# Attention followed by two feed-forward blocks: another order of TensorE's work within a pair of heads, and the low part of x on another engine

## The chip, the cores and the metric

The kernel runs on one core of a Trainium2 chip. The metric is the device time of one execution in microseconds (us), the median of several runs. A profiled execution has its own time and, a little shorter, its span, from the first to the last instruction in the trace.

## The reference

The inputs are q, k and v of shape (2, 12, 448, 64) in float32, a number cap, and four weight matrices in float64. Cut to what matters:

```
scores = cap * tanh(q @ k.T / sqrt(64) / cap)        # each batch and head
attn   = softmax(scores)                              # exp, divided by the row's sum
x      = (attn @ v), heads side by side               # 896 x 768
x      = elu(x @ w_in1) @ w_out1                      # 768 -> 2048 -> 768
out    = relu(x @ w_in2) ** 2 @ w_out2                # 768 -> 2048 -> 768
```

## The kernel before, in words

Every float32 operand of a matrix product is split into a high and a low part (tiles whose names end in h and l), and a product is the sum of three matmuls: high by high, high by low, low by high.

The attention takes the 24 heads as 12 pairs, one iteration of the loop at L505 for each pair n. The 448 keys make three full blocks of 128 per head and a last block that both heads share: seven slots, which `PARTS` (L214) divides into a first part (slots 0 to 3) and a second part (slots 4 to 6). The steps of a pair:

- `turn(n)`, TensorE: eight transposes of k and q into the PSUM tile `pt` (one buffer). `high(n)`, ScalarE: its high part `kqh`. `low(n)`, VectorE: its low part `kql`; for odd n, it also issues the loads of a later group's k and q.
- `scores(n, c)`, TensorE: for c = 0 to 2 six matmuls of 64 rows each, for c = 3 three of 128, into the PSUM tile `sc` (two buffers). `tanh(n, c)`, ScalarE, frees that buffer.
- `exp(n, i)`, ScalarE, in place on part i of the tile `e`.
- `split_p(n, i)`, VectorE: a cast to `ph` (L228) and a subtraction to `pl` (L229). Tile p has one buffer: the first part of a pair waits until all value products of the pair before have read it.
- `prep_v(n)`, GpSimd: for each head a cast (L149) and a subtraction (L150), then a cast (L153) and a subtraction (L154) for the shared block.
- `pv(n, i)`, TensorE: the value products of part i, twelve matmuls each, into the PSUM tile `po` (one buffer). The order of terms is `ph` with `vh`, `ph` with `vl`, `pl` with `vh`. A column of ones in v makes the row sums too.
- `pv_out(n)`, ScalarE copies `po` out, and a DMA fetches the row of sums (`den`). `norm(n)`: VectorE takes the reciprocal (L271), and DMAs write it to DRAM (`far`) and read it back into 64 partitions (`bc`).
- `norm_x(n)`: VectorE multiplies (L291, two instructions of 64 partitions), casts to `xh` (L297), and GpSimd subtracts to `xl` (L298).

All instructions are issued in the order written by hand (`manual_schedule`); each engine, and the DMA queue of SyncE (SP), takes its own in that order. Semaphores order them between engines. In iteration n the engines' orders before are:

- TensorE: `pv(n-1, 1)`, `scores(n, 2)`, `scores(n, 3)`, `pv(n, 0)`, `scores(n+1, 0)`, `scores(n+1, 1)`, `turn(n+2)`
- ScalarE: `tanh(n, 0)`, `high(n+1)`, `tanh(n, 1)`, `exp(n, 0)`, `pv_out(n-1)`, `tanh(n, 2)`, `tanh(n, 3)`, `exp(n, 1)`
- VectorE: `split_p(n-1, 1)`, `low(n+1)`, `norm(n-2)`, `split_p(n, 0)`, `norm_x(n-3)`
- GpSimd: `prep_v(n+1)`, the low part of `norm_x(n-3)`

In iterations 0 and 1 VectorE also prepares the first pieces of w_in1. After the loop come the last value products, mixed with the first products of the feed-forward part, which is TensorE's work for the rest of the time.

Of the kernel before, what the change touches and what calls it, by code (L numbers as in the profile page):

```python
# [26 lines left out]
def attention_moe_kernel(  # L27
# [12 lines left out]
    nc = tc.nc  # L40
# [100 lines left out]
    def prep_v(n):  # L141
        if n >= len(pairs):
            return
        g, pp = divmod(n, 2)
        vh, vl = vhs[n % 2], vls[n % 2]
        for hh in range(2):
            vn = nat[g]["v"][:, 2 * pp + hh]
            h, l = (t[:, hh:NB - 1:2, :D] for t in (vh, vl))
            nc.gpsimd.tensor_copy(h, vn)  # L149
            nc.gpsimd.tensor_tensor(l, vn, h.bitcast(F32), op=ALU.subtract)  # L150
        vn = nat[g]["w"][:, pp]
        h, l = (t[:, NB - 1, :D] for t in (vh, vl))
        nc.gpsimd.tensor_copy(h, vn)  # L153
        nc.gpsimd.tensor_tensor(l, vn, h.bitcast(F32), op=ALU.subtract)  # L154
# [4 lines left out]
    def turn(n):  # L159
        if n >= len(pairs):  # L160
            return
        g, pp = divmod(n, 2)
        hs = slice(2 * pp, 2 * pp + 2)
        pt = ps1.tile([P, 2, W], F32, name="pt", tag="pt")
        for u, src in enumerate("kq"):
            for c in range(NFULL):
                nc.tensor.transpose(  # L167
                    pt[:, u, c * P:(c + 1) * P],
                    nat[g][src][:, c, hs].rearrange("p h d -> p (h d)"),
                    ident,  # L170
                )
            z = kzs[g % 2][:, pp] if u == 0 else qzs[g % 2][:, hs].rearrange("p h d -> p (h d)")
            nc.tensor.transpose(pt[:, u, NFULL * P:], z, ident)
        st["pt", n] = pt

    def high(n, copy=nc.scalar.copy):
        if n >= len(pairs):
            return
        st["qk", n] = [ap_.tile([P, 2, W], F32R, name=x, tag=x) for x in ("kqh", "kql")]
        copy(st["qk", n][0], st["pt", n])  # L180

    def low(n):
        if n >= len(pairs):
            return
        h, l = st["qk", n]
        nc.vector.tensor_tensor(l, st["pt", n], h.bitcast(F32), op=ALU.subtract)
        if n % 2:
            load_group(n // 2 + 2, "kq")

    def scores(n, c):  # L190

        if n >= len(pairs):
            return
        h, l = st["qk", n]
        sc = psc.tile([P, 2, W], F32, name="sc", tag="sc")
        terms = ((h, h), (h, l), (l, h))
        last = len(terms) - 1
        ks = slice(c * P, (c + 1) * P)
        for i, (kt, qt) in enumerate(terms):
            for u, r in enumerate(ROWS if c < NFULL else (slice(0, P),)):  # L200
                nc.tensor.matmul(  # L201
                    sc[:, u, :S], kt[r, 0, ks], qt[r, 1, :S], start=i == 0, stop=i == last
                )
        st["sc", n, c] = sc

    def tanh(n, c):
        if c == 0:
            st["e", n] = ap_.tile([P, NB, S], F32, name="e", tag="e")
        w = 2 if c < NFULL else 1
        nc.scalar.activation(  # L210
            st["e", n][:, 2 * c:2 * c + w], st["sc", n, c][:, :w, :S], AF.Tanh, scale=tsc
        )
# [3 lines left out]
    def exp(n, i):  # L216
        e = st["e", n][:, PARTS[i]]
        nc.scalar.activation(e, e, AF.Exp, scale=capt)  # L218

    def split_p(n, i, copy=nc.vector.tensor_copy):  # L220
        if n < 0:
            return
        if i == 0:
            st["p", n] = [
                ap_.tile([P, NB, S], F32R, name=x, tag=x, bufs=1) for x in ("ph", "pl")
            ]
        e, h, l = (t[:, PARTS[i]] for t in [st["e", n]] + st["p", n])
        copy(h, e)  # L228
        nc.vector.tensor_tensor(l, e, h.bitcast(F32), op=ALU.subtract)  # L229

    def pv(n, i):


        if n < 0:
            return
        if i == 0:
            st["po", n] = ps1.tile([P, 2, W], F32, name="po", tag="po")
        po = st["po", n]
        ph, pl = st["p", n]
        vh, vl = vhs[n % 2], vls[n % 2]  # L240
        terms = ((vh, ph), (vl, ph), (vh, pl))
        mms = [
            (s % 2, slice(0, P), s, x)
            for x in terms for s in range(NB - 1)[PARTS[i]]
        ]
        if i == 1:
            mms += [(u, r, NB - 1, x) for x in terms for u, r in enumerate(ROWS)]
        for j, (u, r, s, (vt, pt)) in enumerate(mms):
            nc.tensor.matmul(  # L249
                po[:, u, :S], vt[r, s], pt[r, s],  # L250
                start=i == 0 and j < 2, stop=i == 1 and j >= len(mms) - 2,
            )

    def pv_out(n, copy=nc.scalar.copy):
        if n < 0:
            return
        pvs = ap_.tile([P, 2, S], F32, name="pvs", tag="pvs", bufs=3)
        copy(pvs, st["po", n][:, :, :S])
        st["pvs", n] = pvs
        den = ap_.tile([D, 2 * S // D], F32, name="den", tag="den")  # L260
        nc.sync.dma_start(den, pvs[D:D + 1].rearrange("p h s -> p (h s)"))
        st["den", n] = den

    def norm(n):


        if n < 0:
            return
        den = st["den", n]
        rd = ap_.tile([D, 2 * S // D], F32, name="rd", tag="rd")  # L270
        nc.vector.reciprocal(rd, den)  # L271
        far = dp.tile([D, 2 * S // D], F32, name="far", tag="far")
        nc.sync.dma_start(far, rd)
        bc = ap_.tile([D, 2, S], F32, name="bc", tag="bc")
        flat = far.rearrange("p s -> (p s)")
        for u in range(2):
            src = flat[u * S:(u + 1) * S].unsqueeze(0).to_broadcast([D, S])
            nc.sync.dma_start(bc[:, u], src)
        st["bc", n] = bc

    def norm_x(n, copy=nc.vector.tensor_copy, low=nc.gpsimd):

        if n < 0:
            return []
        b, hp = pairs[n]
        xn = ap_.tile([P, S], F32, name="xn", tag="xn")
        hi, lo = xh[:, hp, b * S:(b + 1) * S], xl[:, hp, b * S:(b + 1) * S]

        def x():
            for u, r in enumerate(ROWS):  # L290
                nc.vector.tensor_tensor(  # L291
                    xn[r], st["pvs", n][:D, u], st["bc", n][:, u], op=ALU.mult
                )

        return [
            x,
            lambda: copy(hi, xn),  # L297
            lambda: low.tensor_tensor(lo, xn, hi.bitcast(F32), op=ALU.subtract),  # L298
        ]
# [133 lines left out]
    def emit(steps):  # L433
        for step in steps:
            step()
# [42 lines left out]
    with tc.manual_schedule():  # L478
# [26 lines left out]
        for n in range(np_):  # L505
            last = n == np_ - 1
            tanh(n, 0)
            high(n + 1)
            tanh(n, 1)
            split_p(n - 1, 1)  # L510
            exp(n, 0)
            low(n + 1)
            pv(n - 1, 1)
            scores(n, 2)
            scores(n, 3)
            pv_out(n - 1)
            norm(n - 2)
            tanh(n, 2)
            tanh(n, 3)
            exp(n, 1)  # L520
            prep_v(n + 1)
            split_p(n, 0)
            pv(n, 0)
            scores(n + 1, 0)
            scores(n + 1, 1)
            turn(n + 2)
            emit(norm_x(n - 3))
            if n % 2 == 0:
                load_group(n // 2 + 2, "v")

            if n == 0:
                emit(ws.start())
            if n < 2:
                emit(ws.advance())
            if n == 1:
                ws.settle()
# [192 lines left out]
```

## Time and profile before

| what | value |
|---|---|
| median of 3 runs | 622.38 us (621.15 to 623.63) |
| the profiled execution: its time, its span | 621.61 us, 619.8 us |
| busy share of the span: TensorE, VectorE, ScalarE, GpSimd | 94%, 70%, 54%, 13% |
| the same, TensorE, over 95.2 to 105.8 us | 9.04 us of 10.6 |
| mean granted TensorE clock, share of full speed | 0.992 |

The shares are means over the whole span. The attention lies in about the first 146 us of it, the feed-forward blocks in the rest; for one pair of heads, a stretch such as that of the fourth row is to be read. Matmuls are pipelined and their ends are modelled, so TensorE's busy time is not time at its peak rate. A row's duration is an instruction's own, and two neighbours on an engine may overlap by a little, so for sums on one engine the distance between starts is used.

### The profile page before, as it was taken

Reading aid. Unit: us, or ns where it says so; the run is one execution under the profiler, and the core shown is the slowest. Engines: PE = TensorE matmul, PEld = TensorE weight load, DVE = VectorE, ACT = ScalarE, POOL = GpSimd, SP = SyncE. Lnnn points to the kernel's source line nnn. Section 1 sums busy time; section 2 is a strip of 40 time slices with the busy share of each in tenths; the row PEclk is TensorE's granted clock in tenths of the full one; section 3 lists DMA queues with packets and bytes.
Section 4 is the critical chain, followed back from the end, with each engine's and each line's share of the span. In section 5 each row is a group of like instructions: output and inputs, shape, how many; then the busy total and the mean of one; then the engine's idle time right before and its main releaser. Section 6 shows DMA issues by size and latency. Waiting matters only on the chain.

```text
span 619.8 us, 8625 instructions
## 1 busy us (share of the span) xinstructions
PE 585.3 (94%) x3036; PEld 522.5 (84%) x3036; DVE 433.9 (70%) x822; ACT 335.9 (54%) x482; POOL 79.2 (13%) x111
## 2 busy tenths in 40 slices
PE   5788888888899999999999999999999999999997
PEld 3556566656799999999999999999999999999997
DVE  1797888889799888866656666776776779992000
ACT  2777878783498777753332333656666655441000
POOL 1753444432000000000000000000000011231000
PEclk9799999999899999999999999999999999999999
DMA  4853340103444433324333343433334436632000
GB/s 113 215 127 88 79 116 21 30 17 107 144 127 129 128 102 117 96 65 133 104 124 96 112 128 102 128 104 120 108 102 124 119 94 187 186 108 102 22 23 34
DMA packets 82988, 64.76 MB, mean 104 GB/s; under 512 B 38656, under 2 KB 78848, under 8 KB 82944
## 3 DMA queue, kind: packets, MB, share of 16 engines
q1 hardware_dynamic: 82944, 64.20, 35.6%
q8 instruction: 24, 0.39, 0.3%
q14 instruction: 20, 0.16, 0.1%
HBM read 61.34 MB, written 2.80 MB: 103 GB/s over the span
## 4 chain that ended last, share of the span: by engine, by line
PE 81%; DVE 7%; ACT 6%; DMA 2%; SPq 2%; issue 1%; POOL 0%; DVEq 0%; ACTq 0%; POOLq 0%
PE acc L465 18%; PE acc L466 18%; PE acc L464 18%; PE acc L660 6%; PE acc L661 6%; PE acc L659 6%; DVE pl L229 4%; PE po L249 3%; ACT e L218 3%; PE sc L201 2%; DVE ph L228 2%; ACT kqh L180 1%; ACT e L210 1%; PE pt L167 1%; SPq L116 1%
## 5 line engine op out<-in xcount | busy, mean ns | idle before, releaser
L464 PE MATMUL acc<-xh,wh 128*128 128x448 f32 x384 | 140.5, 366 | 3.9 <-ACT wh L407 2.0
L465 PE MATMUL acc<-xl,wh 128*128 128x448 f32 x384 | 140.6, 366 | 0.2 <-DVE xl L298 0.2
L466 PE MATMUL acc<-xh,wl 128*128 128x448 f32 x384 | 140.3, 365 | 0.0
L407 ACT CAST wh<-wf 128x384 fp32r<-128x384 f32 (+2 forms) x114 | 57.8, 507 | 103.4 <-PE acc L465 87.5
L353 ACT ACTIVATE wf<-wst 128x384 f32<-128x384 f32 (+2 forms) x130 | 70.5, 543 | 63.8 <-DVE wl L402 34.4
L402 DVE TENSOR_TENSOR wl<-wf,wh 128x384 fp32r<-128x384 f32 (+2 forms) x116 | 63.6, 548 | 56.1 <-ACT wh L407 56.0
L464 PEld LDWEIGHTS acc<-xh,wh 128*128 128x128 f32 x384 | 72.6, 189 | 10.9 <-ACT wh L407 2.7
L466 PEld LDWEIGHTS acc<-xh,wl 128*128 128x128 f32 x384 | 72.5, 189 | 6.0 <-DVE wl L402 0.7
L465 PEld LDWEIGHTS acc<-xl,wh 128*128 128x128 f32 x384 | 72.5, 189 | 5.5 <-DVE xl L298 0.5
L394 DVE SCALAR_TENSOR_TENSOR wf<-wst,wf 128x384 uint32<-128x384 uint32 (+3 forms) x132 | 71.2, 539 | 0.0
L387 DVE SCALAR_TENSOR_TENSOR wf<-wst,wf 128x384 uint32<-128x384 uint32 (+3 forms) x132 | 71.0, 538 | 0.0
L465 PE MATMUL acc<-gl,wh 128*128 128x448 f32 x192 | 70.0, 365 | 0.0
L466 PE MATMUL acc<-gh,wl 128*128 128x448 f32 x192 | 70.0, 364 | 0.0
L464 PE MATMUL acc<-gh,wh 128*128 128x448 f32 x192 | 69.8, 364 | 0.0
L402 POOL TENSOR_TENSOR late<-wf,late 128x336 fp32r<-128x336 f32 x16 | 15.2, 951 | 388.3 <-ACT late L407 388.3
L366 DVE TENSOR_SCALAR wf<-wf 128x384 uint32<-128x384 uint32 (+3 forms) x132 | 54.4, 412 | 0.6
L210 ACT ACTIVATE e<-sc,tsc 128x896 f32<-128x896 f32 (+1 forms) x48 | 42.6, 917 | 21.8 <-PE sc L201 21.8
L362 DVE TENSOR_SCALAR wf<-wf 128x384 f32<-128x384 f32 (+3 forms) x132 | 46.7, 353 | 8.0 <-ACT wf L353 7.9
L229 DVE TENSOR_TENSOR pl<-e,ph 128x1792 fp32r<-128x1792 f32 (+1 forms) x24 | 51.0, 2125 | 1.6
L646 DVE COPY o<-acc 128x432 f32<-128x432 f32 (+1 forms) x8 | 4.5, 557 | 53.9 <-PE acc L661 47.7
L660 PE MATMUL acc<-wl,gh 128*128 128x432 f32 x112 | 40.3, 359 | 0.0
L661 PE MATMUL acc<-wh,gl 128*128 128x432 f32 x112 | 40.1, 358 | 0.0
(77 smaller groups left out, 993.8 us busy)
## 6 DMA issues: line engine op xcount, KB each, us to landing
wst<-in_moe_w_in_dram SPq DMA_DIRECT2D x64, 384.0 KB, 3.2
wst<-in_moe_w_out_dram SPq DMA_DIRECT2D x24, 384.0 KB, 3.2
wst<-in_moe_w_out_dram SPq DMA_DIRECT2D x16, 432.0 KB, 3.3
wst<-in_moe_w_out_dram SPq DMA_DIRECT2D x16, 336.0 KB, 2.9
wst<-in_moe_w_out_dram SPq DMA_DIRECT2D x12, 256.0 KB, 2.7
bc<-far SPq DMA_DIRECT2D x24, 112.0 KB, 2.9
v<-in_v_dram SPq DMA_DIRECT2D x24, 96.0 KB, 2.6
k<-in_k_dram SPq DMA_DIRECT2D x15, 128.0 KB, 2.7
```

The source lines that it names most:

```text
L229: nc.vector.tensor_tensor(l, e, h.bitcast(F32), op=ALU.subtract)
L353: nc.scalar.activation(self.f[i], hi.bitcast(F32), AF.Abs)
L366: v.tensor_scalar(fb, fb, 3, 0x3FFFFFFF, op0=ALU.logical_shift_left, op1=ALU.bitwise_and)
L387: v.scalar_tensor_tensor(out=fb, in0=hi, scalar=0xC0000000, in1=fb, op0=ALU.bitwise_and, op1=ALU.bitwise_or,)
L394: v.scalar_tensor_tensor(out=fb, in0=lo, scalar=29, in1=fb, op0=ALU.logical_shift_right, op1=ALU.bitwise_or,)
L402: (v if dst is None else nc.gpsimd).tensor_tensor(wl, self.f[i], wh.bitcast(F32), op=ALU.subtract)
L407: (v.tensor_copy if self.alone else nc.scalar.copy)(wh, self.f[i])
L464: nc.tensor.matmul(acc, w[0], x[0], start=first, stop=False)
L465: nc.tensor.matmul(acc, w[0], x[1], start=False, stop=False)
L466: nc.tensor.matmul(acc, w[1], x[0], start=False, stop=last)
L660: nc.tensor.matmul(acc, gh[:, f, gs], w[1], start=False, stop=False)
L661: nc.tensor.matmul(acc, gl[:, f, gs], w[0], start=False, stop=z)
```

## The change

In iteration n, `scores(n, 2)` goes ahead of `pv(n-1, 1)`, and `turn(n+2)` from the end of the iteration to behind `scores(n, 3)`. `scores(n+1, 0)` and `scores(n+1, 1)` go ahead of `pv(n, 0)`. `norm_x(n-3)` goes from behind to ahead of `split_p(n, 0)`, and its subtraction to `xl` from GpSimd to VectorE. ScalarE's order is as it was.

```
             low(n + 1)
+            scores(n, 2)
             pv(n - 1, 1)
-            scores(n, 2)
             scores(n, 3)
+            turn(n + 2)
             pv_out(n - 1)
             norm(n - 2)
             tanh(n, 2)
             tanh(n, 3)
             exp(n, 1)
             prep_v(n + 1)
+            emit(norm_x(n - 3, low=nc.vector))
             split_p(n, 0)
-            pv(n, 0)
             scores(n + 1, 0)
             scores(n + 1, 1)
-            turn(n + 2)
-            emit(norm_x(n - 3))
+            pv(n, 0)
             if n % 2 == 0:
                 load_group(n // 2 + 2, "v")
```

## Rows read from the trace of the kernel before

**Rows 1.** Windows: engines' busy us, TensorE clock (PEclk), DMA share; three stretches.
```profile
19.00:24.00 5.00, 4.45 (x12) 3.81 (x12) 4.79 (x9) 2.96 (x5) 3.06 (x3) 0.50 0.74 167
...
95.20:105.80 10.60, 9.04 (x54) 6.49 (x53) 9.08 (x10) 8.34 (x9) 4.72 (x8) 1.00 0.07 22
...
200.00:600.00 400.00, 400.00 (x2046) 376.40 (x2046) 272.15 (x598) 196.07 (x325) 15.19 (x16) 1.00 0.36 110
```

**Rows 2.** Chain that ended last, one pair: start us, us, what.
```profile
87.54 1.08 PE po L249 x4
88.62 1.42 PE sc L201 x10
...
91.11 1.02 ACT kqh L180
92.12 0.91 ACT e L210
93.06 1.80 ACT e L218
```

**Rows 3.** Timeline of VectorE, one period: start, us, operation, [idle before it].
```profile
94.89 1.12 DVE L228 CAST ph<-e 128x1792 fp32r<-128x1792 f32 x1 [1.33 <-ACT e L218]
96.11 2.02 DVE L229 TENSOR_TENSOR pl<-e,ph 128x1792 fp32r<-128x1792 f32 x1
98.05 1.26 DVE L291 TENSOR_TENSOR xn<-pvs,bc 64x448 f32<-64x448 f32 x2
99.34 0.39 DVE L297 CAST xh<-xn 128x448 fp32r<-128x448 f32 x1
99.65 0.85 DVE L228 CAST ph<-e 128x1344 fp32r<-128x1344 f32 x1
100.54 2.40 DVE L229 TENSOR_TENSOR pl<-e,ph 128x1344 fp32r<-128x1344 f32 x1
102.86 1.21 DVE L186 TENSOR_TENSOR kql<-pt,kqh 128x1024 fp32r<-128x1024 f32 x1
103.99 0.22 DVE L271 RECIPROCAL rd<-den 64x14 f32<-64x14 f32 x1
105.53 1.12 DVE L228 CAST ph<-e 128x1792 fp32r<-128x1792 f32 x1 [1.32 <-ACT e L218]
```

**Rows 4.** Timeline of VectorE, four instructions elsewhere.
```profile
38.19 1.56 DVE L229 TENSOR_TENSOR pl<-e,ph 128x1344 fp32r<-128x1344 f32 x1
...
42.70 2.23 DVE L229 TENSOR_TENSOR pl<-e,ph 128x1792 fp32r<-128x1792 f32 x1
...
52.33 1.09 DVE L228 CAST ph<-e 128x1792 fp32r<-128x1792 f32 x1 [1.37 <-ACT e L218]
...
136.32 1.09 DVE L228 CAST ph<-e 128x1792 fp32r<-128x1792 f32 x1 [1.30 <-PE po L249]
```

**Rows 5.** Timeline of GpSimd, four instructions.
```profile
41.73 1.32 POOL L150 TENSOR_TENSOR vl<-v,vh 128x192 fp32r<-128x192 f32 x1
...
99.82 1.71 POOL L298 TENSOR_TENSOR xl<-xn,xh 128x448 fp32r<-128x448 f32 x1 [3.63 <-DVE xh L297]
103.53 0.34 POOL L149 CAST vh<-v 128x192 fp32r<-128x192 f32 x1 [2.01 <-PE po L249]
103.95 0.60 POOL L150 TENSOR_TENSOR vl<-v,vh 128x192 fp32r<-128x192 f32 x1
```

**Rows 6.** Line L298 on VectorE: ns min/median/max, start, form.
```profile
L298 DVE TENSOR_TENSOR xl<-xn,xh x1: 626/626/626, 160.5 to 160.5; 128x448 fp32r<-128x448 f32 x1
```

**Rows 7.** Timeline of the DMA queue of SP, two issues.
```profile
20.27 0.61 SPq L120 DMA_DIRECT2D qz<-in_q_dram  x1
...
47.03 1.10 SPq L278 DMA_DIRECT2D bc<-far  x2
```

**Rows 8.** DMA issues, KB each, us to landing: 20.26 to 20.9 us; whole span.
```profile
qz<-in_q_dram SPq DMA_DIRECT2D x1, 64.0 KB, 2.7
...
bc<-far SPq DMA_DIRECT2D x24, 112.0 KB, 2.9
```

More of the change, by code (lines that the diff above doesn't have):

```diff
@@ L512, in attention_moe_kernel @@
             low(n + 1)
+            scores(n, 2)
             pv(n - 1, 1)
-            scores(n, 2)
             scores(n, 3)
+            turn(n + 2)
             pv_out(n - 1)
@@ L521, in attention_moe_kernel @@
             prep_v(n + 1)
+            emit(norm_x(n - 3, low=nc.vector))
             split_p(n, 0)
-            pv(n, 0)
             scores(n + 1, 0)
             scores(n + 1, 1)
-            turn(n + 2)
-            emit(norm_x(n - 3))
+            pv(n, 0)
             if n % 2 == 0:
```

## The prediction

> **What bounds the kernel now.** I read the windows first [rows 1]. From 200 to 600 us TensorE is busy all the time and the edit touches nothing there; any gain or loss is made in the loop over pairs and is then carried to the end. In one pair (95.2 to 105.8 us) no engine is full: TensorE 9.04 of 10.6 us, VectorE 9.08, ScalarE 8.34. So a chain through several engines sets the pace.
>
> The chain of waits shows it [rows 2], together with VectorE's timeline [rows 3]. The reader is to follow one round: VectorE ends `pl` of the first part; TensorE does the last four value products (1.08 us), the next pair's scores (1.42) and, until 91.11, the transposes (1.07); ScalarE does `high` (1.02), a tanh (0.92 to the next start) and the exp of the first part (1.80); VectorE casts and subtracts the first part and the round starts again. It closes after 10.64 us, which is the distance of the two casts in [rows 3]. VectorE waits 1.32 us of it for that exp. A second thing stands there: the subtraction of the second part takes 2.40 us where the same form takes 1.56 elsewhere [rows 3, 4]; GpSimd's `xl` (1.71 us) runs just then [rows 5].
>
> **What the order changes in that round.** After the change `scores(n+1, 0)`, `scores(n+1, 1)` and `turn(n+2)` are no longer behind the last term of `pv(n, 0)`. Counted from the end of the first part's `pl`, TensorE now does that last term (1.08), `scores(n+1, 2)` (half of 1.42), then `pv(n, 1)`, whose end releases `pv_out(n)`. ScalarE's `high` and tanh for the next pair depend on matmuls that came half a round earlier, so exp(n+1, 0) can run right behind exp(n, 1). The loop through `pl` and exp is opened; what remains for ScalarE is its own work (8.34) and the wait for `pv_out`. That wait ends about 1.08 + 0.71 + 2.1 = 3.9 us after `pl` (2.1: six full matmuls and three pairs of half ones at the 0.2 us of TensorE's rows, estimated). Then come copy, two tanh and an exp, some 3.7 us (8.34 [rows 1] less 1.02, twice 0.92 and 1.80 [rows 2]), so that exp(n+1, 1) ends at about 7.6, before VectorE asks for it a full round later. ScalarE has about 1 us to spare.
>
> VectorE is then the longest. Its new round, from the distances between starts in [rows 3]: 10.64, less the wait of 1.32, less 2.40 - 1.56 = 0.84 because nothing of GpSimd's `xl` is left beside the second part, plus `xl` on VectorE. That is 0.63 us in the one place where VectorE already does it [rows 6]; an independent successor starts 0.08 before the end (xh at 99.34 with 0.39, next start 99.65), and a dependent one costs 0.12 more than that (0.85 to 0.89), so 0.67. Sum: 9.15 us.
>
> **What x meets in its new place.** Here the trace of before has no row: x and `prep_v` come together. `prep_v(n+1)` starts when `pv(n-1, 1)` has read the old tile, at about 3.1 us after `pl`, and x at about 3.7, behind `split_p(n-1, 1)`, `low` and the reciprocal. Two rows price such a meeting. GpSimd's `xl` costs the second part 0.84 us, though it is only 1.71 long and stands half under the cast before. GpSimd's subtraction at 41.73, 1.32 us where one takes 0.60 undisturbed [rows 5], is followed by a `pl` of 2.23 where it takes 2.02 [rows 3, 4]: 0.21 us. Two such subtractions are 0.42; with 0.08 for the casts I take 0.5 for a round. The bounds are 0 (they pass unnoticed, as the four operations from 103.53 do beside `low`, 1.21 us, and the reciprocal) and 3.0, all of GpSimd's busy time but `xl` (4.72 - 1.71 [rows 1, 5]). I take 0.5 because subtraction beside subtraction is the nearest row.
>
> The Trainium skill ("SBUF — State Buffer", "Who interferes with whom") says that VectorE and GpSimd share one pair of SBUF ports under an exclusive lock, and that a VectorE instruction with two SBUF inputs and a GpSimd one block each other for their whole length. By this rule the sum would be that of the fourth rival below; the trace agrees that they exclude each other (2.40 against 1.56) and not that each operation costs its whole length (0.21 for 0.60).
>
> **Other edits.** x is taken 3.2 us earlier, so it must not wait for its broadcast. One round earlier `norm` has issued it: `den` behind `pv_out` (4.8 us after `pl`), `far`, then two `bc`, landed 2.9 us after their issue [rows 8]. With 0.6 for each issue [rows 7] and 2 us until `far` has landed (an estimate from the 2.9 and 2.7 of [rows 8], which carry more) that is about 11 us after `pl`, and x comes at 3.7 + 9.65 = 13.3. SP's loads of k and q (nine issues of 0.6 us) stand ahead of `den` every second round. They wait for a `turn` that is now earlier, so they start right behind `bc`, at some 8.5, and end at 13.9, before the next `den` at 14.4. The cover is 0.5 us there, and what goes beyond it takes from the 2.3 us that x has. `turn(n+2)` now waits for `low(n+1)` to read `pt`; `low` ends 3.5 us after `pl` and TensorE gets there at 4.6: nothing, with 1 us of cover. Behind it are the scores, which also wait for tanh(n, 2). The buffer of p is read out at 3.9 and rewritten at 6.2: nothing.
>
> **The start.** `turn(2)` is now ahead of `scores(1, 0)` and `pv(0, 0)`, and the last tile that it transposes lands at 20.27 + 2.7 = 23.0 us [rows 7, 8]. TensorE stands until then, and then works at 1.2 GHz for some us, as it did from 19 to 24 [rows 1]. Estimated with matmuls at 0.37 us for 4.7 us, `pv(0, 1)` ends at 32.1, and `split_p(1, 0)` starts there. Two rounds of VectorE without x (2 x 6.9 by the distances in [rows 3]) and an estimated 4.3 for the weights that it prepares and a wait for exp(2, 1) bring it to x of pair 0 at about 50.2; each us beyond 50.5 would count in full. Its broadcast was issued at 47.03, the second half 0.55 later [rows 7], and lands at 50.5, so x waits there anyway. With x (1.29), xh, xl and the port's 0.5, the cast of pair 3 starts at 53.0 and not at 52.33 [rows 4]: a loss of 0.7.
>
> **The sum.** From the cast of pair 3 to that of pair 11 it took 136.32 - 52.33 = 83.99 us [rows 4]. Now there are seven rounds of 9.15 + c, c being the port's price, and one without `low` (1.13 less) and without `prep_v`: 8.02. The gain is 83.99 - 64.05 - 8.02 - 0.7 = 11.2 - 7c. With c = 0.5 it is 7.7 us. From pair 11's `pl` to the end TensorE's order is as before, and its stalls there hang on `pv_out` and the weights, so I add nothing. The profiled execution was 621.61, so 613.9; the median is 0.77 above it, so 614.7.
>
> **The rivals.** All times are for the median.
> - *The port costs next to nothing* (c = 0). For it: the casts and `low` of before show no sign of GpSimd. Against: 0.21 and 0.84. 622.4 - 11.2 = 611.2.
> - *TensorE becomes the bound.* It is busy 9.04 us of a round, and its idle time before (1.56) is not all the wait for exp. Now it waits in order for `low`, tanh(n, 2), `ph` and `pl`; if it keeps 1.1 us of waits the round is about 10.2, the gain 11.2 - 7 x 1.05 = 3.9, and the time 618.5. Against it: each of these waits is over by my sums with 0.5 us or more to spare.
> - *No gain:* the cast still waits for exp, because ScalarE, in order, is held in `pv_out` and so late with the next pair. For it: its 8.34 us. Then 621 to 623.
> - *Slower: x in front of the split pays for GpSimd in full.* x, xh and xl now stand on the path that sets the end, and each of the four operations on the heads' v blocks one of them for its length, 2 x (0.34 + 0.60) = 1.88 [rows 5]: 11.2 - 13.2 = -1.9, so 624.3. It decides from c = 1.6 on. The skill's page named above gives this rule. For it: GpSimd's 1.32 and 1.71, which are mostly waiting; against it: 0.21.
>
> **Chances.** My forecast 0.50, the free port 0.17, TensorE 0.15, no gain 0.06, slower 0.12. A measurement of this kernel can tell about 0.5% (3.1 us) from no change. Faster by more: 0.50 + 0.17 + most of TensorE's (0.11) = 0.78; within: 0.11; slower: 0.11. The range goes down a little below the free port, 610.5, and up past TensorE's case, 620.5; outside are no gain, slower, and a few in a hundred below. The forecast's own range, with c from 0.2 to 0.9, is 612.5 to 617.5.
>
> **What would show it.** Right: the cast of the first part waits no longer for exp; the distance of two such casts is 9.4 to 10.0 us; the second part's `pl` is 1.56; x or xl are a few tenths longer than 0.63, or start after a gap, when GpSimd subtracts; the chain of waits runs along VectorE. Wrong: `ph` still waits on exp; x waits for `bc` after pair 0; VectorE idle while TensorE is full; rounds above 10.6; or a start that is later than 53.0 at pair 3.

## The result

The changed kernel took 612.89 us (median of 4 runs, 612.53 to 615.70) against 623.0 us for the kernel before beside it; the ratio is 0.9851, with a 95% interval of 0.9813 to 0.9889. A second set of six runs on another chip gave 613.68 us and 0.988 (0.9856 to 0.9903). Forecast were 614.7 us and a range of 610.5 to 620.5. The profiled execution took 612.95 us with a span of 611.1, against 621.61 and 619.8: 8.7 us less. Of all runs below, one (619.49 us) counts as slow, and no reading rests on it.

The window of the changed kernel for one round (columns as in [rows 1]):

```profile
92.37:101.98 9.61, 9.14 (x55) 6.61 (x55) 9.37 (x12) 8.30 (x9) 4.21 (x7) 1.00 0.10 26
```

A round is 9.61 us and no longer 10.64. VectorE is busy for 9.37 of it, TensorE for 9.14. In VectorE's timeline the round looks so:

```profile
92.37 1.12 DVE L228 CAST ph<-e 128x1792 fp32r<-128x1792 f32 x1
93.60 2.03 DVE L229 TENSOR_TENSOR pl<-e,ph 128x1792 fp32r<-128x1792 f32 x1
95.54 0.85 DVE L228 CAST ph<-e 128x1344 fp32r<-128x1344 f32 x1
96.43 1.56 DVE L229 TENSOR_TENSOR pl<-e,ph 128x1344 fp32r<-128x1344 f32 x1
97.90 1.22 DVE L186 TENSOR_TENSOR kql<-pt,kqh 128x1024 fp32r<-128x1024 f32 x1
99.03 0.22 DVE L271 RECIPROCAL rd<-den 64x14 f32<-64x14 f32 x1
99.18 1.49 DVE L291 TENSOR_TENSOR xn<-pvs,bc 64x448 f32<-64x448 f32 x2
100.70 0.42 DVE L297 CAST xh<-xn 128x448 fp32r<-128x448 f32 x1
101.16 0.90 DVE L298 TENSOR_TENSOR xl<-xn,xh 128x448 fp32r<-128x448 f32 x1
101.98 1.12 DVE L228 CAST ph<-e 128x1792 fp32r<-128x1792 f32 x1
```

Beside [rows 3] the reader is to see four things. No row carries an idle time: the wait of 1.32 us for exp is gone. The second part's subtraction is 1.56 and not 2.40. Two instructions are longer than they need be: x takes 1.49 for its two instructions (1.26 in [rows 3]), and xl 0.90 where VectorE's lone xl took 0.63 [rows 6]. And GpSimd's timeline shows what runs beside them, stretched itself (undisturbed: 0.34 and 0.60, [rows 5]):

```profile
99.26 0.93 POOL L150 TENSOR_TENSOR vl<-v,vh 128x192 fp32r<-128x192 f32 x1
100.14 0.74 POOL L149 CAST vh<-v 128x192 fp32r<-128x192 f32 x1
```

The chain of waits of the changed kernel goes through other steps than [rows 2]:

```profile
90.22 0.91 ACT pvs L258
91.13 0.93 ACT e L210
92.06 0.04 issue
92.10 1.49 PE sc L201 x12
...
93.60 2.04 DVE pl L229
95.63 0.04 issue
95.68 1.07 PE po L249 x4
96.75 0.80 PE sc L201 x5
97.55 2.24 PE po L249 x12
```

High and exp are no longer in it. It runs from the copy of `po` through a tanh, the scores and the value products of both parts back to the next copy, and passes VectorE only at the `pl` of the first part. That does not say that VectorE waits there: `pl` starts 0.11 us after the end of the cast ahead of it, where [rows 3] has 0.10. Which of the two ways sets the round is shown by the runs without GpSimd's preparation of v, below.

**Where the 8.7 us came from.** The casts of pairs 3 and 11, which [rows 4] has at 52.33 and 136.32, are now here:

```profile
53.48 1.48 DVE L228 CAST ph<-e 128x1792 fp32r<-128x1792 f32 x1
...
129.07 1.08 DVE L228 CAST ph<-e 128x1792 fp32r<-128x1792 f32 x1
```

Between them lie 75.59 us, against 83.99: 8.40 gained. Pair 3 comes 1.15 later. From the cast of pair 11 to the end it takes 482.03 us against 483.48, 1.45 less. 8.40 - 1.15 + 1.45 = 8.7.

Two of these terms need a second look. Between the two casts lie one round of 10.09, six of 9.60 and a last one of 7.89 without `low`. And in the profiled execution of the second set (615.6 us, a span of 613.7) the same kernel has its cast of pair 11 here:

```profile
129.71 1.08 DVE L228 CAST ph<-e 128x1792 fp32r<-128x1792 f32 x1
```

Pair 3 came at 54.00, 1.67 later than before, and the way to pair 11 was 75.71 us, a gain of 8.28. From there to the end it took 483.99 us, 0.51 more than before. So the gain up to pair 11 is seen twice, 7.25 and 6.61 us. The 1.45 behind it is seen once.

### The profile page after: what moved, and what is told of

Same layout as the page of the kernel before. It is cut to its first block, busy times and chain, and to the rows that moved or that the text cites. A ratio compares the mean times of both kernels' runs of the same rounds, so it can differ in the third digit from the quotient of the medians.

```text
span 611.1 us, 8631 instructions
## 1 busy us (share of the span) xinstructions
PE 587.5 (96%) x3036; PEld 523.6 (86%) x3036; DVE 435.8 (71%) x831; ACT 334.5 (55%) x482; POOL 76.2 (12%) x102
## 4 chain that ended last, share of the span: by engine, by line
PE 86%; DVE 5%; ACT 3%; DMA 2%; SPq 2%; issue 1%; POOL 0%; DVEq 0%; ACTq 0%
PE acc L465 19%; PE acc L466 18%; PE acc L464 18%; PE po L249 7%; PE acc L660 6%; PE acc L659 6%; PE acc L661 6%; PE sc L201 4%; DVE pl L229 3%; ACT pvs L258 1%; ACT e L210 1%; SPq L116 1%; DMA v<-in_v_dram 1%; DMA wst<-in_moe_w_in_dram 1%; SPq L125 0%
## 5 line engine op out<-in xcount | busy, mean ns | idle before, releaser
L229 DVE TENSOR_TENSOR pl<-e,ph 128x1792 fp32r<-128x1792 f32 (+1 forms) x24 | 43.3, 1804 | 1.6
```

## The experiments

Two theories stood at first. A: TensorE's new order opens the loop through exp, after which VectorE's own instructions and the price of the port set the round. B: the moved x makes the gain. A round is read here as the distance between the casts of the first part of neighbouring pairs in VectorE's timeline, in the middle of the attention.

### TensorE's order alone

```
             prep_v(n + 1)
-            emit(norm_x(n - 3, low=nc.vector))
             split_p(n, 0)
             scores(n + 1, 0)
             scores(n + 1, 1)
             pv(n, 0)
+            emit(norm_x(n - 3))
```

> TensorE's new order alone; x stays behind the split of p, and its low part on GpSimd. Theory A (the new order opens the loop through exp, and VectorE's own work then sets the round): VectorE's round of before, 10.64, less its wait of 1.32 is 9.32; GpSimd's preparation of v now meets the split and adds 0 to 0.4, so 9.3 to 9.7 us a round, and no wait for a broadcast at pair 3: 611 to 615 us. Theory B (the moved x makes the gain, because it fills VectorE's wait and takes GpSimd's subtraction off the second part): the order alone leaves a round of 10.2 or more, 619 to 622 us.

Measured: 617.53 us, ratio 0.9926 (0.9901 to 0.9950), a round of 9.91. The round is nearer to A than to B, but above both of A's bounds, and the time is outside A's range. In VectorE's timeline the wait for exp is gone, and the price of GpSimd is larger than thought:

```profile
95.02 1.66 DVE L291 TENSOR_TENSOR xn<-pvs,bc 64x448 f32<-64x448 f32 x2
```

x is 0.40 longer than in [rows 3], and the second part's `pl` keeps its 2.40, which is 0.84 above 1.56. At the cast of pair 11 the order alone has gained 4.83 us of the change's 7.25, about two thirds; where x and its low part stand decides the rest. The medians, of which the order has about half, also hold what comes behind pair 11.

### x alone

```
             prep_v(n + 1)
+            emit(norm_x(n - 3, low=nc.vector))
             split_p(n, 0)
             pv(n, 0)
             scores(n + 1, 0)
             scores(n + 1, 1)
             turn(n + 2)
-            emit(norm_x(n - 3))
```

> x ahead of the split and its low part on VectorE; TensorE's order as before. Theory A: low still waits for high, which waits for the transposes behind the last value term, so x comes 5.9 us after the first part's subtraction and the split at about 8.2, where exp would have let it start at 7.4: a round of 11.4 to 11.7 and 628 to 632 us. Theory B: x lies in the wait of 1.32 us and the second part is 0.84 shorter: a round of 10.0 to 10.6, 614 to 622 us.

Measured: 634.99 us, ratio 1.0209 (1.0179 to 1.0240). Rounds are 11.7 and 12.7 to 12.9 us. B falls: the moved x without the new order costs 13 us. A has the direction and the shorter rounds; its time, 628 to 632 us, was too low. VectorE's timeline shows the step that A named, `low` waiting for `high`, with x behind it at 88.14:

```profile
86.85 1.23 DVE L186 TENSOR_TENSOR kql<-pt,kqh 128x1024 fp32r<-128x1024 f32 x1 [3.40 <-ACT kqh L180]
```

The windows show what the longer rounds have that the shorter ones have not:

```profile
66.21:77.88 11.67, 8.87 (x53) 6.59 (x53) 9.13 (x12) 8.37 (x9) 3.14 (x6) 1.00 0.33 81
77.88:90.65 12.77, 10.11 (x53) 7.89 (x53) 9.13 (x12) 8.37 (x9) 3.15 (x6) 0.87 0.31 73
```

With the same work, TensorE's mean granted clock is 0.87 in the longer one, and it is busy 1.24 us longer; from 80 to 82 us its granted clock is 0.50, that is 1.2 GHz, after it had been busy for 1.35 of the 4 us before. VectorE and ScalarE are as busy in both. So the rounds at full clock are as A expected (11.4 to 11.7), and the longer ones hold a stretch at 1.2 GHz. Why it comes in some rounds only stays open: from 64 to 68 us TensorE was busy for no more, 1.36 of 4 us, and its clock stayed at 1.00.

### The transposes alone, and the next pair's scores alone

Each from the kernel before; first the transposes:

```
             scores(n, 3)
+            turn(n + 2)
...
             scores(n + 1, 1)
-            turn(n + 2)
```

> Of the change only the transposes of pair n+2 go behind scores(n, 3); the rest as before. Theory A: the loop keeps the last value term (1.08), one score block (0.71), tanh, high, tanh and exp (4.7) and the split (3.2): 9.8 us a round, 613 to 616 us. Theory B: the transposes are not what holds exp, 10.4 or more, 620 to 623 us.

Measured: 620.15 us, ratio 0.9975 (0.9951 to 1.0000), a round of 10.09. The loop is shorter, but VectorE still waits 0.52 for exp in each round, and GpSimd's preparation now lies beside the first part's `pl` (2.23 for 2.02). The expected 9.8 left that out. The round lies between A's 9.8 and B's 10.4; the time is in B's range.

```
             split_p(n, 0)
-            pv(n, 0)
             scores(n + 1, 0)
             scores(n + 1, 1)
+            pv(n, 0)
             turn(n + 2)
```

> Of the change only the next pair's first two score blocks go ahead of pv(n, 0); transposes and x as before. Theory A: the loop is last value term (1.08), transposes (1.07), high, tanh, exp (3.8), split (3.2), 9.2 us, less than VectorE's 9.3 to 9.7, which sets the round: 611 to 615 us, as with the whole order. Theory B: 10.4 or more, 620 to 623 us.

Measured: 622.58 us, ratio 1.0004 (0.9988 to 1.0020), a round of 10.54: no gain, as B had it, and A's number was wrong. The chain shows what I had left out:

```profile
94.70 0.88 ACT pvs L258
95.59 0.92 ACT e L210
...
96.55 1.50 PE sc L201 x10
98.05 2.63 PE po L249 x12
100.67 0.33 PE pt L167 x3
...
101.58 1.02 ACT kqh L180
...
105.24 0.89 ACT pvs L258
```

ScalarE takes its work in order. The copy of `po` stands behind exp, and the tanh that frees the PSUM tile for the next scores stands behind the copy. With the scores ahead of `pv(n, 0)` and the transposes still behind it, the way copy, tanh, scores, value products, transposes, high, tanh, exp, copy closes after 10.54 us. So neither move does much alone; together they take the transposes out of that way too.

### The port's price taken away

```
-            prep_v(n + 1)
+            if n == 0:
+                prep_v(n + 1)
```

> The changed kernel, with GpSimd's preparation of v left out from pair 2 on, so that later pairs use old tiles of v. Theory A (c, the price of the shared port, is what lengthens x and xl): the first x instructions and xl fall to 0.6 each, the round from 9.60 to 9.1, and the time by about 7 x 0.5 and a little at pair 3, to 608 to 610 us. Theory C (x and xl are longer there for a reason of their own): they and the 9.60 stay, 612 to 614 us.

Measured: 609.61 us, ratio 0.9796 (0.9770 to 0.9823), rounds of 9.06 to 9.12. VectorE's timeline:

```profile
87.11 1.20 DVE L291 TENSOR_TENSOR xn<-pvs,bc 64x448 f32<-64x448 f32 x2
88.34 0.39 DVE L297 CAST xh<-xn 128x448 fp32r<-128x448 f32 x1
88.77 0.63 DVE L298 TENSOR_TENSOR xl<-xn,xh 128x448 fp32r<-128x448 f32 x1
89.31 1.09 DVE L228 CAST ph<-e 128x1792 fp32r<-128x1792 f32 x1
90.50 2.03 DVE L229 TENSOR_TENSOR pl<-e,ph 128x1792 fp32r<-128x1792 f32 x1
92.56 0.86 DVE L228 CAST ph<-e 128x1344 fp32r<-128x1344 f32 x1
```

x falls from 1.49 to 1.20 and xl from 0.90 to 0.63. So theory C, that they are longer for a reason of their own, falls. The round is 0.5 shorter, but that is not the whole price: between the last two rows lie 2.06 us and no longer 1.94 (93.60 to 95.54 in the changed kernel), as VectorE now waits for the exp of the second part. Without that wait its round would be about 9.0, and the price of GpSimd's preparation about 0.6.

### The next bound

```
-            emit(norm_x(n - 3, low=nc.vector))
+            emit(norm_x(n - 3, low=nc.vector)[:2])
+            if n == 1:
+                nc.gpsimd.memset(xl.bitcast(F32), 0.0)
```

together with the edit of the run above.

> As the run without the preparation of v, and the subtraction to xl is left out of the loop as well (xl is filled with zeros once, in iteration 1). VectorE's own round would be 8.5 us. Theory A (the next bound is the loop pv_out, tanh, two score blocks, pv of both parts with a score block between them: 0.91 + 0.92 + 1.50 + 2.64 + 0.80 + 2.24 and gaps = 9.07, as the changed kernel's chain shows from pair 2 to 4): the round stops at 9.07, 608 to 610 us, about as without the preparation alone. Theory D (VectorE alone sets the round): it follows to 8.5 us, 603 to 606 us.

Measured: 608.83 us, ratio 0.9788 (0.9765 to 0.9812), rounds of 9.03 to 9.17. VectorE has 0.6 us less to do, and the round is as with it. Its timeline has a wait again, and the chain runs through ScalarE and TensorE alone:

```profile
88.44 0.91 ACT pvs L258
89.36 0.91 ACT e L210
...
90.31 1.48 PE sc L201 x12
91.79 2.64 PE po L249 x12
...
97.49 0.91 ACT pvs L258
```

The loop closes after 9.05 us. This is the second bound, 0.5 us under the first; D, that VectorE alone counts, falls. The rounds of the run above, 9.06 to 9.12, lie at it too.

### The low part of x on the one engine or the other

The low part back on GpSimd, x still ahead of the split:

```
-            emit(norm_x(n - 3, low=nc.vector))
+            emit(norm_x(n - 3))
```

> The changed kernel with the subtraction to xl back on GpSimd, behind the preparation of v. Theory A: VectorE saves 0.8, but GpSimd's xl stands beside the split of the first part and takes 0.8 from it: 9.5 to 9.8 us a round, 612 to 616 us. Theory D (VectorE's own instructions alone count): 8.8 us, then the loop through pv_out at 9.07, 608 to 610 us.

Measured: 609.53 us, ratio 0.9801 (0.9777 to 0.9825), a round of 9.07, 3.4 us less than the change. A's price did not come, and D's 9.07 did; its reason, that VectorE's own instructions alone count, is not shown by it. GpSimd's timeline, and then VectorE's, show why A's price did not come:

```profile
93.02 2.47 POOL L298 TENSOR_TENSOR xl<-xn,xh 128x448 fp32r<-128x448 f32 x1
```

```profile
92.91 1.56 DVE L229 TENSOR_TENSOR pl<-e,ph 128x1344 fp32r<-128x1344 f32 x1
94.40 1.21 DVE L186 TENSOR_TENSOR kql<-pt,kqh 128x1024 fp32r<-128x1024 f32 x1
```

xl is held back while the second part's `pl` runs at its full pace, and is then done beside `low`, which reads PSUM and is not longer for it (1.21 as in [rows 3]). Other instructions of VectorE are longer here: the first part's cast takes 1.23 and its `pl` 2.22, for 1.12 and 2.02 in [rows 3], and VectorE has no wait. Its round with these prices is 9.07 and the loop through the copy of `po` 9.05, so these runs do not tell which of the two holds it.

x behind the split, its low part on VectorE:

```
             pv(n, 0)
+            emit(norm_x(n - 3, low=nc.vector))
```

and the line ahead of `split_p(n, 0)` taken out.

> TensorE's new order and xl on VectorE, but x behind the split of the first part. Theory A: the round with the order alone was 9.91; less 0.84 of the second part, plus 0.55 to 0.67 for xl: 9.6 to 9.75, and no wait for a broadcast at pair 3: 612 to 616 us. Theory B (x has to be ahead of the split): 9.9 or more, 616 to 619 us.

Measured: 615.14 us, ratio 0.9893 (0.9862 to 0.9924), a round of 9.73: as A expected. Beside it the place of x is worth 0.13 us a round (9.73 to 9.60), and its low part on VectorE 0.18 (9.91 to 9.73). These prices do not add up over other pairs of edits: with the low part on GpSimd, the run before this one, the place of x is worth 0.84 (9.91 to 9.07).

### Again, side by side

Four kernels on one chip: the change; the kernel with the low part of x on GpSimd and x ahead of the split; and that kernel with one more edit each, the transposes of pair 2 back at the end of iteration 0, or `scores(n, 2)` back behind `pv(n - 1, 1)`.

```
-            turn(n + 2)
+            if n > 0:
+                turn(n + 2)
...
             pv(n, 0)
+            if n == 0:
+                turn(n + 2)
```

and

```
-            scores(n, 2)
             pv(n - 1, 1)
+            scores(n, 2)
             scores(n, 3)
```

> The changed kernel once more, beside the three that follow: 612 to 614 us, rounds of 9.60. It is the yardstick for them.

Measured: 613.68 us, ratio 0.9880 (0.9856 to 0.9903), rounds of 9.60.

> The subtraction to xl back on GpSimd, once more. Theory A, mended (GpSimd's xl costs nothing where VectorE runs low, which reads PSUM, so the round falls to the loop through pv_out): rounds of 9.07 and 608.5 to 610.5 us, 2.5 to 4.5 less than the changed kernel. If the first result was an accident of its chip: within 1 us of the changed kernel.

Measured: a median of 613.21 us, ratio 0.9864 (0.9825 to 0.9904), but from runs of 608.37, 609.63, 611.68, 614.74, 616.92 and 619.49 us. The profiled execution, of 608.37, has rounds of 9.03 to 9.10, as A expected; the median is within 1 us of the change, as the rival expected. So the gain of 3.4 us is there in some executions and not in others.

> As the run before, and in iteration 0 alone the transposes of pair 2 go back to the end. Theory A (the start is gated at pair 3 by the broadcast, which hangs on the load queue): the split of pair 1 starts 1 to 2 us earlier, but that of pair 3 only 0 to 0.5 earlier, so 608 to 610.5 us, no difference to the run before that can be told. Theory E (TensorE's stand for the last tile of pair 2 costs what it lasts): pair 3 comes 1 us or more earlier and the time falls by as much.

Measured: 615.49 us, ratio 0.9903 (0.9883 to 0.9923). On the start A is right: the split of pair 1 starts at 29.59 and not at 31.4 to 31.6, that of pair 3 at 51.57 and not at 51.75 to 52.04. But the rounds are 9.98, which neither theory had, so the time says nothing on the start.

> xl on GpSimd, and scores(n, 2) back behind pv(n-1, 1). The loop through pv_out is then shorter by 0.8 (8.3), and TensorE's own work in a round is about 8.9. Theory A (VectorE's sum with the port's price is at 9.07 too, without a gap): the round stays at 9.0 to 9.1, 608.5 to 610.5 us. Theory D (the loop through pv_out alone held it): 8.9 and about 1.2 us less than with scores ahead.

Measured: 615.22 us, ratio 0.9899 (0.9880 to 0.9919). Both expectations missed. The trace tells what happens: the round to pair 4 is 9.07, the next 10.34, and from then on 9.98 each. In its later rounds GpSimd's timeline and VectorE's read:

```profile
93.06 3.00 POOL L298 TENSOR_TENSOR xl<-xn,xh 128x448 fp32r<-128x448 f32 x1
```

```profile
93.02 2.02 DVE L229 TENSOR_TENSOR pl<-e,ph 128x1792 fp32r<-128x1792 f32 x1
94.97 1.82 DVE L228 CAST ph<-e 128x1344 fp32r<-128x1344 f32 x1
```

The same GpSimd instruction now starts beside the first part's `pl`, and the cast behind it is 0.97 us longer (0.85 to 1.82). The kernel with xl on GpSimd has two patterns that repeat themselves, 9.07 and 9.98 a round: the run before this one differs from the run with xl on GpSimd and no further edit in iteration 0 alone, and has 9.98 from pair 3 on. That small shifts at the start decide which pattern it falls into, and that the slower executions of the unchanged order are in the longer one, fits this, but was not shown, as none of those was profiled. Neither of the last two edits can be judged by these runs. The change as it is has been seen in one pattern only (9.60, in both profiled executions). Which of the two is better is therefore open; xl on GpSimd is not a safe improvement.

## Why the prediction was right

- *What bounds the kernel, and what the order changes.* Right. VectorE no longer waits for exp, and VectorE's own row of instructions has no gap. One of the signs did not come: the chain of waits does not run along VectorE; that VectorE sets the round rests on its row without a gap and on the run without the preparation. That both moves on TensorE are needed, and not the one or the other, the prediction did not see; the two runs with one move each showed it.
- *VectorE's round of 9.15 and the port's 0.5.* 9.65 was forecast, 9.60 measured. That it is so near is partly luck, as both terms were off and their errors nearly cancel: without the preparation VectorE's own round is about 9.0, 0.15 under the forecast, and the price about 0.6, 0.1 over it. The price sits where it was put: 0.29 at x, under a subtraction and a cast of GpSimd, and 0.27 at xl. Of the rivals, the free port is out by that run, and so is the one where each operation costs its whole length: GpSimd's four instructions were 1.88 us long and took about 0.6. The trace agrees with the exclusive lock on the ports that VectorE and GpSimd share, as the Trainium skill states it ("SBUF — State Buffer", "Who interferes with whom"). To price it at each operation's whole length was the step that failed in that rival. What is waited for is the rest of the other's instruction, as the last of the runs above shows: when the cast of 0.85 started at 94.97, GpSimd's subtraction had 1.09 us left, and the cast took 0.97 longer.
- *The rival that TensorE becomes the bound.* Not the bound, but next: the loop through the copy of `po` closes at 9.05, so that of VectorE's 9.60 only 0.5 could be had by relieving VectorE. The prediction did not add up this loop. One of its steps was also summed wrong: six full matmuls and three pairs at 0.2 us are 1.8 and not 2.1, and the chain has 2.24.
- *The start.* By the prediction's own list a start later than 53.0 at pair 3 was a sign of being wrong, and it came at 53.48, and at 54.00 in the second profiled execution: 1.15 and 1.67 later than before and not 0.7. The direction was right, and so was the step to `split_p(1, 0)`, which started at 32.16 (32.1 forecast). But VectorE reached x of pair 0 at 50.77, and x did not wait for its broadcast, which was to hold it until 50.5; from there to the cast it took 2.71 and not 2.5. That the transposes of pair 2 are not what delays pair 3 is shown by the run that puts them back, with xl on GpSimd: 2 us earlier at pair 1, at most 0.5 at pair 3. With x behind the split pair 3 came at 51.80, and with x ahead of it and only its low part on GpSimd at 51.75. So the low part on VectorE has a share in the delay; the rest, as VectorE was also 0.6 us earlier there (50.19 and 50.17 for 50.77), was not separated.
- *From pair 11 to the end.* The term was put at nothing. It was 1.45 us in one profiled execution and -0.51 in the other, so no gain of the edit is shown there, and what the first adds to the 7.25 is luck. Windows of 3 us show one thing that differs: one of the kernel before, one of the changed kernel, and one of its second profiled execution:

```profile
161.00:164.00 3.00, 2.81 (x9) 2.52 (x9) 3.00 (x9) 1.07 (x2) 0.00 (x0) 0.50 0.05 14
```

```profile
147.00:150.00 3.00, 3.00 (x10) 2.65 (x9) 1.32 (x3) 0.23 (x1) 1.16 (x1) 0.50 0.04 11
```

```profile
154.00:157.00 3.00, 2.51 (x7) 2.00 (x8) 2.71 (x7) 0.87 (x3) 0.00 (x0) 0.69 0.17 56
```

All three executions have a stretch of some 3 us at 1.2 GHz (granted clock 0.50; the last window holds it only in part). In the kernel before it came after TensorE had stood 1.93 us for the last pair's x, and in the second execution of the changed kernel after it had stood 2.40 us for it. In the first it came after a wait of 2.22 us for weights, ahead of the arrival of that x at 153 us, for which TensorE had to wait anyway. So the same kernel has it in either place, and the edit did not decide it. That the stretch makes the whole difference of 1.96 us between the two executions was not shown.

The sum was 7.7 us and is 8.7 in the first profiled execution: rounds 8.42 forecast (83.99 - 64.05 - 3.5 - 8.02) and 8.40 found, start -0.7 and -1.15, end 0 and 1.45. In the second it is 6.1: 8.28, -1.67 and -0.51. The forecast lies between the two. The rounds agree so well because a longer first one (10.09 for 9.65) is made up by six of 9.60 and a last of 7.89 for 8.02.

## What to carry to other kernels

Write each engine's work of one round as a sum, and close the loops between engines as a second set of sums, with every in-order engine's queue in them: the round is the largest, and the next largest says what the next edit can give. A move that opens one loop may do nothing alone when a second loop runs through the same steps; try the moves one by one and together. When two engines exclude each other at SBUF, look for a neighbour that reads PSUM, and mistrust a gain that hangs on where in the round the other engine's instruction happens to start.

## What the runs showed of the hardware that had not been expected

- With the same instructions in the same order on VectorE and GpSimd, GpSimd's subtraction to xl cost VectorE nothing (2.47 us, held back beside `pl` and done beside `low`) or 0.97 us (3.00 us, ended within a cast). Executions of one kernel with it lay between 608.4 and 616.9 us.
- `low`, which reads PSUM, took 1.21 to 1.23 us in every run, whatever GpSimd did beside it.
- Where a stretch at 1.2 GHz falls can differ between two executions of one kernel: ahead of the last pair's x in one (147 to 150 us), behind it in the other (from 154 us on). The time from pair 11 to the end was 482.03 us in the first and 483.99 in the second.
- With TensorE's order as before and x moved, the stretch came in some rounds and not in others: 12.77 us at a mean granted clock of 0.87, 11.67 at 1.00.
